# Linear attention with decay and a bilinear FFN on one core: the second pair's loads, scalings, transposes and order of products are changed

## The chip, the cores and the metric

The kernel runs on one core of a Trainium2 chip. The metric is the device time of one execution in microseconds (us). A core has five engines that run beside each other, each in the order of its own instructions: TensorE (PE in the profile; PEld is its loading of weights), VectorE (DVE), ScalarE (ACT), GpSimd (POOL) and SyncE (SP), which here issues nearly all transfers. An instruction waits on semaphores for what it needs, and everything behind it on its engine waits with it. SBUF is the memory that the engines work on; PSUM, eight banks of 2 KB a partition, takes TensorE's results.

## The reference

Two stages. The first is attention with a state that decays, for 4 batches, 8 heads, 768 tokens and 64 values a head; the second a bilinear FFN on all 3072 tokens.

```python
gamma = 1.0 - 2.0 ** (-5.0 - np.arange(H))
for t in range(S):
    state = gamma * state + einsum('bhd,bhe->bhde', k[:, :, t], v[:, :, t])
    y[:, :, t] = scale * einsum('bhd,bhde->bhe', q[:, :, t], state)
x = y.transpose(0, 2, 1, 3).reshape(B * S, H * D)      # 3072 x 512
out = ((x @ w_a) * (x @ w_b)) @ w_out                  # 512 -> 1536 -> 512
```

## The kernel before, in words

**The attention, by chunks.** Tokens are taken in slots of 128 (24 slots, six to a batch). The decay is put into k and q beforehand: `scaled` (L203) multiplies the raw tile by a table and writes bf16 into `kqb`. v is only cast to bf16 (`vb`). Then, for each slot: the scores, a product of k and q transposed (`at`); their masking on VectorE into `aT`; the state (`st` in PSUM), to which a product of k and v is added; a bf16 copy of the state; and `y`, the sum of an inter product (old state with q) and an intra product (masked scores with v). `y` is copied as bf16 into `xt`, the FFN's input, tokens along the free side.

**The first six slots go in pairs.** For batch 0, `load_pair` (L93) loads 256 tokens of k, q or v at once, 512 KB: partition p holds tokens 2p and 2p+1 ("par" 0 and 1). So a tile of parity par holds every second token. `casts2` (L331) does a pair's scalings and v's casts, with the engine named for k and q, and v's casts on GpSimd right behind. `flip2` (L339) transposes k and q on TensorE into PSUM and copies them to SBUF: `kT2` by parity, `qT2` with the two parities woven together, so that its tokens stand in order. `scores2` (L354) multiplies k of one parity with q of all 256 tokens in halves c of 128 tokens and masks the result with `masks[par]`. `update2(u, c)` (L373) adds half c of a pair to the state; `keep_state` (L390) copies the state to `gbd[1 - c]` with two ScalarE instructions. `inter2` (L394) multiplies `gbd[c]` with q, `intra2` (L405) v with the masked scores, and `leave2` (L417) casts `ys[u][c]` into `xt`. `warm` (L429) is a product of zeros that nothing reads; it keeps TensorE occupied. From slot 6 on the slots are handled one at a time, from slot 10 on with transposes made by transfers.

**PSUM.** The pool `psff` has three buffers, handed out in turn to transposes, scores of one parity, and all FFN products; `psat` and `psst` hold the other scores, `y` and the state.

**The order is written out by hand.** `seq` (L73) ties each instruction to the one before it on its engine, so lines 508 to 581 are the order on every engine for the three pairs and the FFN's first tile, in which `ffn_a` (a = x w_a, copied to `asb` by ScalarE) and `ffn_g` (g = x w_b, times `asb` on VectorE into `ht`) run over 12 blocks ft of 128. For ft 0 and 1 they run on half of the tile's columns at a time: the first 256 columns are pair 0's tokens, the others pair 1's. The weights are cast to bf16 on GpSimd (`cast_w`, `cast_o`) as they land. From L584 `run` follows for the other tiles, with `turn` for the attention of later slots in between and `ffn_out` (L472) for the outputs.

**The queue of transfers.** `LOADS` (L21) is the order of the first loads on SP's queue; `issue_loads(6)` issues the first entries at L123, the rest comes at L542. Later loads are issued by `casts` behind the transposes of a slot. A transfer waits for the one eight places before it in the program's order, as they share a semaphore in turn; that counts the stores too, of which the first six are issued by SP and the later ones by ScalarE, behind the copy of the output that they store.

## Time and profile before

| What | us |
|---|---|
| median of 3 timed executions | 233.76 (233.73 to 234.46) |
| the profiled execution, its own time | 235.14 |
| span of its instructions | 233.40 |
| TensorE busy in the span | 226.59 |
| VectorE, ScalarE, GpSimd busy | 95.65, 84.53, 77.43 |

The columns of the page are explained where they are used. In an order of time, a row has the start in us, the length in us, the engine, the line of the kernel, the operation, the tiles as output<-input, the shape, how many instructions are merged into the row, and in brackets how long the engine had been idle before and what released it. A table of stretches has, for each, its length, then the busy time of PE, PEld, DVE, ACT and POOL with the count of instructions, the clock granted to TensorE (1.00 is full), the share of the transfer engines and GB/s. A row of groups has the busy time and the mean of one in ns, then the idle time before them. Rows that begin with a start and a length and have no tile's shape are pieces of the chain of waits: the work that ended last, followed back.

### The profile page before, as it was taken

The numbers are of one execution on the slowest core, as the hardware profiler recorded it, in microseconds if no ns is written. First come the engines' busy times: TensorE is split into PE (matmuls) and PEld (weight loads), VectorE is DVE, ScalarE is ACT, GpSimd is POOL, SyncE is SP. The second block draws the span as 40 slices with busy tenths as digits, with TensorE's granted clock in tenths as the row PEclk, the third lists the DMA queues.
The fourth block names the chain that finished last, engine by engine and source line by source line (L and its number), as shares of the span: only waits on it lengthen the run. The fifth ranks groups of instructions, "written<-read, shape, count | busy, mean of one in ns | idle before, by whom it ended". The sixth has DMA issues, their size and how long they took to land.

```text
span 233.4 us, 5089 instructions
## 1 busy us (share of the span) xinstructions
PE 226.6 (97%) x2094; PEld 125.8 (54%) x2094; DVE 95.7 (41%) x170; ACT 84.5 (36%) x166; POOL 77.4 (33%) x100
## 2 busy tenths in 40 slices
PE   7999999999999999999799999999999999999995
PEld 6667445686554444545354544454544444445874
DVE  3785267543642274614164630164720233310530
ACT  3454436342134433414244523353422343322422
POOL 4347666788664336444454530000000000000000
PEclk9999999999999999999999999999999999999999
DMA  6999999999999999999999972200002200012102
GB/s 173 290 332 352 341 278 361 363 212 222 204 195 263 277 217 228 177 220 220 249 243 203 234 113 90 93 1 3 0 3 90 90 0 3 0 45 90 48 0 90
DMA packets 91894, 38.59 MB, mean 165 GB/s; under 512 B 71776, under 2 KB 87392, under 8 KB 91872
## 3 DMA queue, kind: packets, MB, share of 16 engines
q1 hardware_dynamic: 89280, 33.69, 64.8%
q10 hardware_dynamic: 2592, 4.59, 5.9%
q8 instruction: 16, 0.26, 0.5%
q14 instruction: 6, 0.05, 0.1%
HBM read 28.31 MB, written 6.29 MB: 148 GB/s over the span
## 4 chain that ended last, share of the span: by engine, by line
PE 74%; DMA 10%; SPq 7%; POOL 3%; ACT 1%; issue 1%; DVE 1%; ACTq 0%; POOLq 0%
PE g L456 22%; PE a L446 21%; PE o L481 19%; DMA kf<-in_k_dram 8%; SPq L223 4%; PE idle L432 4%; SPq L91 3%; POOL kqb L209 3%; DMA qf<-in_q_dram 2%; PE at L252 1%; PE y L297 1%; PE y L412 1%; PE tp L348 1%; PE st L268 1%; PE at L364 1%
## 5 line engine op out<-in xcount | busy, mean ns | idle before, releaser
L458 DVE TENSOR_TENSOR ht<-g,asb 128x512 bf16<-128x512 f32 (+1 forms) x86 | 52.0, 605 | 108.9 <-PE g L456 83.7
L456 PE MATMUL g<-xt,wb_bf 128*128 128x512 bf16 (+1 forms) x344 | 75.4, 344 | 1.6 <-ACT asb L449 1.4
L446 PE MATMUL a<-xt,wa_bf 128*128 128x512 bf16 (+1 forms) x344 | 75.9, 345 | 0.4 <-DVE xt L181 0.3
L449 ACT CAST asb<-a 128x512 bf16<-128x512 f32 (+1 forms) x86 | 44.2, 517 | 72.2 <-PE a L446 69.1
L481 PE MATMUL o<-wo_bf,ht 128*128 128x512 bf16 (+2 forms) x312 | 64.2, 363 | 0.0
L456 PEld LDWEIGHTS <-wb_bf 128*128 128x128 bf16 x344 | 33.6, 98 | 30.2 <-issue 2.1
L446 PEld LDWEIGHTS <-wa_bf 128*128 128x128 bf16 x344 | 32.7, 98 | 28.1 <-DVE xt L181 0.6
L481 PEld LDWEIGHTS <-ht 128*128 128x128 bf16 x312 | 29.2, 98 | 31.5
L209 POOL TENSOR_TENSOR kqb<-kf,ktab 128x512 bf16<-128x512 f32 x22 | 22.9, 1043 | 33.9 <-DMA kf<-in_k_dram 33.4
L179 ACT COPY osb<-o 128x512 f32<-128x512 f32 (+2 forms) x25 | 14.1, 565 | 53.5 <-PE o L481 41.5
L257 DVE TENSOR_TENSOR aT<-at,mask 128x512 bf16<-128x512 f32 x36 | 22.3, 682 | 0.0
L209 POOL TENSOR_TENSOR kqb<-qf,qtab 128x512 bf16<-128x512 f32 x18 | 18.8, 1043 | 3.9 <-DMA qf<-in_q_dram 3.1
L181 POOL CAST vb<-vf 128x512 bf16<-128x512 f32 x24 | 14.5, 612 | 11.6 <-DMA vf<-in_v_dram 9.8
L432 PE MATMUL idle<-zero 128*128 128x256 f32 x30 | 10.4, 487 | 1.6 <-DVE zero L125 1.3
L306 ACT CAST xt<-y 128x512 bf16<-128x512 f32 x18 | 9.7, 589 | 3.0 <-PE y L297 3.0
L432 PEld LDWEIGHTS idle<-zero 128*128 128x128 f32 x30 | 6.7, 243 | 2.9 <-DVE zero L125 1.2
L370 DVE TENSOR_TENSOR aT<-at,mask 128x512 bf16<-128x512 f32 x12 | 7.4, 683 | 1.2 <-PE at L364 1.2
L181 POOL CAST wa_bf<-wsta 128x1024 bf16<-128x1024 f32 (+1 forms) x7 | 6.4, 920 | 3.5 <-DMA wsta<-in_moe_w_a_dram 3.5
L181 POOL CAST wb_bf<-wstb 128x1024 bf16<-128x1024 f32 (+1 forms) x7 | 6.4, 920 | 3.4 <-DMA wstb<-in_moe_w_b_dram 3.4
L181 POOL CAST wo_bf<-wsto 128x1024 bf16<-128x1024 f32 x6 | 6.3, 1042 | 2.4 <-DMA wsto<-in_moe_w_out_dram 2.4
L179 ACT CAST gst<-st 128x256 bf16<-128x256 f32 x12 | 4.5, 372 | 6.7 <-PE st L268 6.7
L252 PE MATMUL at<-kqT 64*64 64x128 bf16 x288 | 5.8, 219 | 0.0
(51 smaller groups left out, 86.8 us busy)
## 6 DMA issues: line engine op xcount, KB each, us to landing
kf<-in_k_dram SPq DMA_DIRECT2D x18, 256.0 KB, 4.3
qf<-in_q_dram SPq DMA_DIRECT2D x18, 256.0 KB, 4.9
vf<-in_v_dram SPq DMA_DIRECT2D x18, 256.0 KB, 5.0
out_dram<-osb ACTq DMA_DIRECT2D x17, 256.0 KB, 2.0
wsta<-in_moe_w_a_dram SPq DMA_DIRECT2D x6, 512.0 KB, 8.7
wstb<-in_moe_w_b_dram SPq DMA_DIRECT2D x6, 512.0 KB, 8.7
wsto<-in_moe_w_out_dram SPq DMA_DIRECT2D x6, 512.0 KB, 9.4
kf<-in_k_dram SPq DMA_DIRECT2D x3, 512.0 KB, 7.1
```

The source lines that it names most:

```text
L179: seq(nc.scalar.copy(dst, src))
L181: seq(engine.tensor_copy(dst, src))
L209: seq(eng.tensor_tensor(dst, src, tab, op=ALU.mult))
L223: seq(nc.sync.dma_start_transpose(out=kqT[t].rearrange("p a b c -> p (a b) c"), in_=kqb[t].rearrange("p a hp r d -> p (a hp r d)")))
L257: seq(nc.vector.tensor_tensor(aT[t][:, r], at[r], mask.to_broadcast([P, HP, P]), op=ALU.mult))
L306: seq(nc.scalar.copy(xt[J][:, 2 * r : 2 * r + 2, i * P : (i + 2) * P].rearrange("p j (s n) -> p j s n", s=2), ys[t // 2][r].rearrange("p ( ...
L432: seq(nc.tensor.matmul(idle[:, : 2 * P], zero[:, :P], zero, start=True, stop=True, skip_group_check=True))
L446: seq(nc.tensor.matmul(a, wa_bf[:, kt, fs], xcols(J, kt, c0, c1), start=(kt == 0), stop=(kt == KT - 1)))
L449: seq(nc.scalar.copy(asb, a))
L456: seq(nc.tensor.matmul(g, wb_bf[:, kt, fs], xcols(J, kt, c0, c1), start=(kt == 0), stop=(kt == KT - 1)))
L458: seq(nc.vector.tensor_tensor(ht[J][:, ft, c0:c1], g, asbs.pop((J, ft, c0)), op=ALU.mult))
L481: seq(nc.tensor.matmul(o, ht[J][:, ft, i * P : (i + 1) * P], wo_bf[:, ft, c0:c1], start=(ft == 0), stop=(ft == NFT - 1)))
```

## The change

Names and lines here are those of the kernel before.

- The first loads are listed one by one, and k of pair 1 goes ahead of v of pair 0: k0, q0, k1, v0, q1, v1.
- GpSimd scales k of pair 1 first and casts v of pair 0 after that; q of pair 1 is scaled by VectorE (parity 0) and GpSimd (parity 1), where VectorE did both.
- `flip2` keeps q's transposes by parity, as k's, so that the copies write side by side; `scores2` and `inter2` read q with the two parities one after the other; the masks are built in that order; `leave2` weaves the parities together as it writes `xt`.
- The order by hand: after pair 0's scores come pair 1's k transposes, and pair 0's and pair 1's products are interleaved anew; the state copies for pair 0 come later; all products of pair 1 stand before the first `ffn_a`, and one warm-up product of a single call is left out. One copy of pair 0's `y` is on VectorE instead of ScalarE.

```diff
-LOADS = "p0 p1 w0 w1 w2 w3 w4 p2 w5 o0 ... s11".split()
+LOADS = "k0 q0 k1 v0 q1 v1 w0 w1 w2 w3 w4 k2 q2 v2 w5 o0 ... s11".split()
...
-    issue_loads(6)
+    issue_loads(10)
...
-                                        base=-par, pattern=[[0, 1], [1, P]],
+                                        base=-par, pattern=[[0, 1], [1, 2], [2, 64]],
...
     def casts2(u, on):
-        for t in (2 * u, 2 * u + 1):
-            new_nat(t)
+        if 2 * u not in kqb:
+            for t in (2 * u, 2 * u + 1):
+                new_nat(t)
         for (i, par), eng in on.items():
-            scaled(eng, 2 * u + par, i)
-        for t in (2 * u, 2 * u + 1):
-            cast(nc.gpsimd, vb[t], raws["v", t])
+            t = 2 * u + par
+            if i == V:
+                cast(eng, vb[t], raws["v", t])
+            else:
+                scaled(eng, t, i)
...
     def flip2(u, i, on):
-        if i == 1 and u not in qT2:
-            qT2[u] = tra.tile([P, HP, P, 2], BF16, tag="qT2", name="qT2", bufs=2)
+        into = (kT2, qT2)[i]
+        if u not in into:
+            into[u] = tra.tile([P, 2, HP, P], BF16, ...)
...
-                cast(eng, qT2[u][:, :, :, pars[0]], tp[:, 0])
+            cast(eng, into[u][:, pars[0] : pars[0] + len(pars)], tp)
...
-                                         qT2[u][half(r), hp, half(c), :],
+                                         qT2[u][half(r), :, hp, half(c)],
...
-                                         qT2[u][:, hp, half(c), :], start=False, stop=False,
+                                         qT2[u][:, :, hp, half(c)], start=False, stop=False,
...
-            cast(eng, xt[J][:, i + c], ys[u][c])
+            cast(eng, xt[J][:, i + c].rearrange("p k (m par) -> p k par m", par=2),
+                 ys[u][c].rearrange("p k (par m) -> p k par m", par=2))
...
     casts2(0, {(K, 1): D_, (K, 0): D_, (Q, 0): D_, (Q, 1): D_})
+    casts2(1, {(K, 0): G_, (K, 1): G_})
+    casts2(0, {(V, 1): G_, (V, 0): G_})
...
     scores2(0, 1)
     scores2(0, 0, True)
+    warm(2, psat, "y1")
+    flip2(1, K, [((0, 1), A_)])
+    intra2(0, 1, True)
     update2(0, 0)
-    warm(2, psat, "y1")
-    casts2(1, {(K, 0): G_, (K, 1): G_, (Q, 0): D_, (Q, 1): D_})
+    intra2(0, 0, False)
+    casts2(1, {(Q, 0): D_, (Q, 1): G_, (V, 0): G_, (V, 1): G_})
+    flip2(1, Q, [((0,), D_)])
+    inter2(0)
+    flip2(1, Q, [((1,), A_)])
+    leave2(0, (D_, A_))
     update2(0, 1)
-    intra2(0, 1, True)
-    inter2(0)
-    intra2(0, 0, False)
-    flip2(1, K, [((0, 1), A_)])
-    leave2(0, (A_, A_))
-    flip2(1, Q, [((0,), D_), ((1,), D_)])
-    warm(1, psff, "ff")
     scores2(1, 0, True)
     scores2(1, 1)
+    warm(2, psff, "ff")
     update2(1, 0)
+    intra2(1, 0, True)
+    inter2(1)
+    update2(1, 1, False)
+    intra2(1, 1, False)
+    leave2(1, (A_, D_))
     cast_w(0, 2)
     W2 = 2 * P
-    warm(2, psff, "ff")
-    update2(1, 1, False)
-    intra2(1, 0, True)
-    inter2(1)
     ffn_a(0, 0, 0, W2)
-    intra2(1, 1, False)
-    leave2(1, (A_, D_))
     ffn_a(0, 1, 0, W2)
...
+    ffn_a(0, 1, W2, 2 * W2)
     ffn_g(0, 1, 0, W2)
-    ffn_a(0, 1, W2, 2 * W2)
...
-            casts2(2, {(K, 0): G_, (K, 1): G_})
+            casts2(2, {(K, 0): G_, (K, 1): G_, (V, 0): G_, (V, 1): G_})
```

More of the change, by code (lines that the diff above doesn't have):

```diff
@@ L18 @@
 ON_PE = 10
-LOADS = "p0 p1 w0 w1 w2 w3 w4 p2 w5 o0 o1 o2 o3 o4 o5 s6 s7 s8 s9 s10 s11".split()
+LOADS = "k0 q0 k1 v0 q1 v1 w0 w1 w2 w3 w4 k2 q2 v2 w5 o0 o1 o2 o3 o4 o5 s6 s7 s8 s9 s10 s11".split()
 @with_exitstack
@@ L91, in load_slot, with load_pair @@
             seq(nc.sync.dma_start(out=raws[nm, t], in_=s))
-    def load_pair(u):
-        for nm, src in (("k", k), ("q", q), ("v", v)):
-            f = raw.tile([P, H, 2, D], F32, tag=nm + "f", name=nm + "f")
-            s = src[0, :, 2 * u * P : 2 * (u + 1) * P, :].rearrange("h (p two) d -> p h two d", two=2)
-            seq(nc.sync.dma_start(out=f, in_=s))
-            for par in range(2):
-                raws[nm, 2 * u + par] = f[:, :, par, :]
+    def load_pair(nm, u):
+        src = {"k": k, "q": q, "v": v}[nm]
+        f = raw.tile([P, H, 2, D], F32, tag=nm + "f", name=nm + "f")
+        s = src[0, :, 2 * u * P : 2 * (u + 1) * P, :].rearrange("h (p two) d -> p h two d", two=2)
+        seq(nc.sync.dma_start(out=f, in_=s))
+        for par in range(2):
+            raws[nm, 2 * u + par] = f[:, :, par, :]
     def load_w(j):
@@ L118, in issue_loads @@
             what = pending.pop(0)
-            {"p": load_pair, "s": load_slot, "w": load_w, "o": load_o}[what[0]](int(what[1:]))
+            if what[0] in "kqv":
+                load_pair(what[0], int(what[1:]))
+            else:
+                {"s": load_slot, "w": load_w, "o": load_o}[what[0]](int(what[1:]))
     kqb = {}
-    issue_loads(6)
+    issue_loads(10)
     zero = const.tile([P, 2 * P], F32, name="zero")
@@ L331, in casts2 @@
     def casts2(u, on):
-        for t in (2 * u, 2 * u + 1):
-            new_nat(t)
+        if 2 * u not in kqb:
+            for t in (2 * u, 2 * u + 1):
+                new_nat(t)
         for (i, par), eng in on.items():
-            scaled(eng, 2 * u + par, i)
-        for t in (2 * u, 2 * u + 1):
-            cast(nc.gpsimd, vb[t], raws["v", t])
+            t = 2 * u + par
+            if i == V:
+                cast(eng, vb[t], raws["v", t])
+            else:
+                scaled(eng, t, i)
     def flip2(u, i, on):
-        if i == 0 and u not in kT2:
-            kT2[u] = tra.tile([P, 2, HP, P], BF16, tag="kT2", name="kT2", bufs=2)
-        if i == 1 and u not in qT2:
-            qT2[u] = tra.tile([P, HP, P, 2], BF16, tag="qT2", name="qT2", bufs=2)
+        into = (kT2, qT2)[i]
+        if u not in into:
+            into[u] = tra.tile([P, 2, HP, P], BF16, tag="kq"[i] + "T2", name="kq"[i] + "T2", bufs=2)
         for pars, eng in on:
```

5 lines of the change are left out of this document (1 added, 4 removed).

## The prediction

> **What bounds the kernel now.** I read the page's busy times and its chain of waits first, then the stretches, then the order of time on each engine in the two places where TensorE is not full.
>
> ```profile
> span 233.4 us, 5089 instructions
> PE 226.6 (97%) x2094; PEld 125.8 (54%) x2094; DVE 95.7 (41%) x170; ACT 84.5 (36%) x166; POOL 77.4 (33%) x100
> PE 74%; DMA 10%; SPq 7%; POOL 3%; ACT 1%; issue 1%; DVE 1%; ACTq 0%; POOLq 0%
> ...
> 100.00:150.00 50.00, 48.76 (x426) 23.69 (x425) 16.76 (x27) 16.85 (x31) 18.70 (x21) 1.00 0.96 190
> 150.00:200.00 50.00, 50.00 (x388) 23.90 (x387) 18.98 (x29) 18.56 (x34) 0.00 (x0) 1.00 0.06 22
> ```
>
> TensorE is busy 97%, in the two stretches shown at full clock (the 1.00). But the chain is only 74% TensorE: 17% of it is transfers and SP's queue. From 150 us on TensorE is full; the one hole after 24 us lies between 100 and 150 (48.76 of 50). The change works on the first 23 us, where warm-up matmuls hide the waits. So there are two questions: what the front gains, and whether the hole swallows it. The chain at the hole, then PE and ACT there:
>
> ```profile
> 109.18 5.36 DMA qf<-in_q_dram
> 114.61 0.34 ACTq L491
> 114.99 0.59 ACT asb L449
> ...
> 115.63 1.02 PE L456 MATMUL g<-xt,wb_bf 128*128 128x512 bf16 x4 [1.24 <-ACT asb L449]
> ...
> 111.83 0.59 ACT L179 COPY osb<-o 128x512 f32<-128x512 f32 x1 [2.00 <-PE o L481]
> 114.99 0.59 ACT L449 CAST asb<-a 128x512 bf16<-128x512 f32 x1 [2.57 <-DMA qf<-in_q_dram]
> ```
>
> The output copy ends at 112.42, its store stands behind it on ScalarE's queue, and the store is issued only when a load of q, issued at 109.18, has landed (114.54). The asb copy queued behind the store holds g: TensorE loses 1.24 us. Nothing later on TensorE waits, so the end is 114.54 plus fixed work, whenever TensorE comes there earlier, and also when it comes up to 1.24 us later. What sets 114.54 is the train of loads, transposes and stores on SP's queue. The change swaps two entries of that queue (k of pair 1 and v of pair 0, equal sizes) and leaves its other entries and their order alone.
>
> **The front, part by part.** Times are those of the trace.
>
> ```profile
> 8.64 0.70 PE L432 MATMUL idle<-zero 128*128 128x256 f32 x2
> 9.63 0.64 PE L364 MATMUL at<-qT,kT 64*64 64x128 bf16 x32 [0.29 <-DVE qT L181]
> 15.22 0.76 PE L364 MATMUL at<-qT,kT 64*64 64x128 bf16 x32
> 19.28 0.61 PE L446 MATMUL a<-xt,wa_bf 128*128 128x256 bf16 x4
> 20.18 0.61 PE L446 MATMUL a<-xt,wa_bf 128*128 128x256 bf16 x4 [0.29 <-DVE xt L181]
> ...
> 8.84 0.73 DVE L181 COPY qT<-tp 128x512 bf16<-128x512 bf16 x1 [0.60 <-PE tp L348]
> 10.10 2.48 DVE L370 TENSOR_TENSOR aT<-at,mask 128x512 bf16<-128x512 f32 x4 [0.53 <-PE at L364]
> ...
> 10.55 0.76 ACT L392 CAST gbd<-st 64x256 bf16<-64x256 f32 x2 [1.69 <-PE st L383]
> 13.53 1.01 ACT L179 COPY kT<-tp 128x1024 bf16<-128x1024 bf16 x1 [0.80 <-PE tp L348]
> ...
> 8.72 1.17 POOL L181 CAST vb<-vf 128x512 bf16<-128x512 f32 x2 [4.77 <-DMA vf<-in_v_dram]
> 10.62 2.04 POOL L209 TENSOR_TENSOR kqb<-kf,ktab 128x512 bf16<-128x512 f32 x2 [0.73 <-DMA kf<-in_k_dram]
> ...
> 4.95 1.74 SPq L97 DMA_DIRECT2D qf<-in_q_dram  x1
> qf<-in_q_dram SPq DMA_DIRECT2D x1, 512.0 KB, 7.3
> ...
> 16.23 1.06 PE idle L432 x4
> 17.89 0.57 PE y L400 x16
> 19.00 0.40 PE y L412 x16
> 21.66 0.44 PE a L446 x4
> ```
>
> These are, in this order, TensorE, VectorE, ScalarE, GpSimd, the issue of pair 1's q with its time to landing, and four pieces of the chain.
>
> *Transposes by parity.* The copy out of PSUM now writes side by side instead of every second element.
>
> ```profile
> L458 DVE TENSOR_TENSOR ht<-g,asb 128x512 bf16<-128x512 f32 x58 | 40.1, 691 | 86.4 <-PE g L456 72.2 <-ACT asb L449 14.2
> L458 DVE TENSOR_TENSOR ht<-g,asb 128x256 bf16<-128x256 f32 x28 | 11.9, 425 | 22.6 <-PE g L456 11.5 <-ACT asb L449 11.1
> L238 DVE COPY kqT<-tp 128x1024 bf16<-128x1024 bf16 x4 | 2.8, 689 | 3.6 <-PE tp L236 3.6
> L179 ACT COPY qT<-tp 128x512 bf16<-128x512 bf16 x2 | 1.5, 738 | 0.5 <-PE tp L348 0.5
> L179 ACT COPY kT<-tp 128x512 bf16<-128x512 bf16 x2 | 1.1, 588 | 1.9 <-PE tp L348 1.9
> ```
>
> On ScalarE that is 738 to 588 ns. On VectorE the two ht rows give (691 - 425)/256 = 1.04 ns an element and 159 ns fixed; kqT, 1024 elements side by side, has (689 - 159)/1024 = 0.52 ns. So qT with 512 takes about 159 + 265 = 424 ns instead of 730 (bounds: 345, half of kqT's row, and no gain). The scores of pair 0 then start at 9.34, when the warm-up matmuls end, not at 9.63: -0.29, and aT ends at 12.30 instead of 12.58. The strided write moves to xt, 588 to 738 ns at worst; the a products of the first half cover it (0.88 us on TensorE), or it costs 0.15.
>
> *k ahead of v.* GpSimd gets k when it got v, 8.72, and is done at 10.76; v follows to 11.93, two microseconds later than now. Its readers are queued later as well: the scores (0.64) end at 9.98, the warm-ups (1.06) at 11.0, k's transposes at about 11.6, ScalarE's kT copy (1.01) at 12.6, and the state copies of keep_state (0.76) stand behind it, to 13.4, where now they end at 11.31. inter2(0) waits for those; behind it on TensorE stands the second half of q's transposes.
>
> *q on two engines.* q lands at 4.95 + 7.3 = 12.25, unmoved. The likely price comes from these rows (DVE, then POOL):
>
> ```profile
> 34.05 0.82 DVE L209 TENSOR_TENSOR kqb<-qf,qtab 128x512 bf16<-128x512 f32 x1
> 12.50 1.32 DVE L209 TENSOR_TENSOR kqb<-qf,qtab 128x512 bf16<-128x512 f32 x2
> 35.39 0.68 DVE L458 TENSOR_TENSOR ht<-g,asb 128x512 bf16<-128x512 f32 x1
> ...
> 32.27 2.04 POOL L209 TENSOR_TENSOR kqb<-kf,ktab 128x512 bf16<-128x512 f32 x2 [0.69 <-DMA kf<-in_k_dram]
> ```
>
> VectorE's scaling began at 34.05 while GpSimd's ran to 34.31, and took 0.82, where the pair at 12.50 took 0.66 each: it ended 0.55 after GpSimd did, as if it had stood still until then. Side by side the two halves may thus come one after the other.
> (a) GpSimd first, 12.35 to 13.39; VectorE ends at 13.94; transposes 14.35, inter2 14.6, second half 14.9, ScalarE's copy 0.59, scores of pair 1 at 15.55: +0.33 on 15.22.
> (b) VectorE first, 13.03, GpSimd (1.04) 14.07, transposes 14.45, copy 15.05, scores 15.1: -0.1.
> (c) No exclusion: GpSimd 13.39, inter2 done 13.85, transposes 14.1, copy 14.7, scores 14.77: -0.45.
> I take (a), since both times that the trace shows the pair it is VectorE that stands.
>
> [...]
>
> *All products first.* From the scores of pair 1 to the first a of the second half (15.22 to 20.18) TensorE has the same work, in another order. Now the last a before it starts at 19.28 and needs 0.44, so 0.46 is waiting for xt, which goes, since two a (0.88) stand behind the last intra while xt is copied (0.69 to 0.74). New is a wait inside inter2(1): its state update now follows the warm-up, and its copies (0.76 and about 0.1 of hand-over) have only intra (0.40) and the first half of inter (0.29) as cover: 0.17. Uncovered whole it would be 0.86. Net -0.3. The masking of aT, 2.48 long, ends before its last reader as now.
>
> Front in all: (a) 0.0, (b) -0.4, (c) -0.75. A further limit stands at pair 2:
>
> ```profile
> 36.20 0.78 PE L348 MATMUL tp<-ident,kqb 128*128 128x128 bf16 x8
> 37.09 1.02 PE L456 MATMUL g<-xt,wb_bf 128*128 128x512 bf16 x4
> ```
>
> The transposes at 36.20 need the PSUM buffer that ht frees at 35.39 + 0.68 = 36.07, and that ht follows the scaling tied to k's landing at 32.2, which doesn't move. After 36.07 only ScalarE's chain shortens, so g at 37.09 can come to about 36.6: at most -0.5 goes on. At 115 the 0.0 to 0.5 meets the unmoved 114.54: the 1.24 us wait becomes up to 1.74.
>
> Sum: 233.4 span + 0.0 = 233.4. The profiled execution took 235.14 (1.74 around its span), the median without a profile is 233.76; no change there too, rounded **233.7**.
>
> **Rivals.** *R1, the hole is not there without a profile.* The profiled execution is 1.38 longer than the median, nearly the hole's 1.24; against it, the instants of the loads come from kernel queues that are the same in both. Then the front goes through: 233.76 - 0.0 to 0.5, 233.3 to 233.7.
> *R2, faster.* (c) holds, the hole is absent, and pair 2 gives way as well (its scaling is no longer beside GpSimd's k if the transfers run quicker): 233.76 - 0.75 = 233.0. Its case is weakened by the 0.82 row.
> *R3, slower: a store overtakes the load.* ScalarE issues the third store of this block at 109.86, 0.68 after the q load at 109.18. If TensorE arrives over 0.68 earlier, 256 KB stand ahead of that load:
>
> ```profile
> 108.00:114.50 6.50, 6.39 (x30) 2.81 (x29) 0.01 (x1) 1.17 (x2) 2.05 (x3) 1.00 1.03 185
> ```
>
> at 185 GB/s that is 1.4 us, and 114.54 becomes 115.9: 235.1. The limit of 0.5 at pair 2 speaks against it.
> *R4, the split does not do what it says.* By (a) q takes 1.04 + 0.55 = 1.59 instead of 1.32; the gain of the other parts is spent on it. It ends at 233.7 with or without the hole, so it is inside the forecast.
>
> **How the numbers follow.** What a measurement of this kernel can tell from no change is about 0.3%, 0.70 us: same is 233.06 to 234.46. The hole absorbs (with R4): 0.47. R1: 0.14. R2 and larger gains: 0.22. R3, or a train of transfers that is later for another reason: 0.17. From the first two nearly all is same, 0.59; faster 0.23, slower 0.18. The likeliest case alone has 233.3 to 234.1; with the top of R2 and about half of R3's price, 232.9 to 234.5.
>
> **What would show it.** Right: the wait before g near 115 grows by what the front gains, the q load still lands near 114.5, and the end stands. For the front: VectorE's qT copy near 0.42; GpSimd's and VectorE's q scalings, one of them longer than its 1.04 or 0.66; the scores of pair 1 at 15.1 to 15.6; the first a of the second half at 19.8 to 20.2. Wrong: no wait near 115 and an end shorter by the front's gain, or a load of q that lands elsewhere than at 114.5 by more than 0.5.

## The result, and the profile after

| | before | after |
|---|---|---|
| median of 20 timed executions, us | 234.08 | 234.70 |
| shortest | 233.58 | 234.59 |
| profiled execution, its own time (span) | 235.14 (233.4) | 234.88 (233.2) |

The ratio is 1.0028, with a 95% interval of 1.0015 to 1.0041: the change made the kernel 0.6 us slower, where 233.7 and no change had been forecast. Single executions lie up to 1.9 us apart for before and 0.9 for after, and one of each, some 4 us longer, is left out of the ratio, so the shortest of each, 1.01 us apart, is shown beside the median.

The page of after: span, busy times, the engines' shares of the chain of waits, and two groups (busy us, mean ns, idle time ahead and what ended it).

```profile
span 233.2 us, 5085 instructions
PE 226.5 (97%) x2092; PEld 126.3 (54%) x2092; DVE 94.4 (41%) x169; ACT 84.5 (36%) x166; POOL 78.8 (34%) x101
PE 94%; DVE 2%; ACT 1%; issue 1%; ACTq 0%
L449 PE MATMUL a<-xt,wa_bf 128*128 128x512 bf16 (+1 forms) x344 | 75.7, 345 | 0.5 <-DVE ht L461 0.4
```

The chain is TensorE for 94%, where 17% had been transfers and SP's queue: the wait of 1.24 us near 115 is gone. TensorE's busy time is the same, and yet the span is only 0.2 less. The stretches of after say where TensorE stood instead (length, then busy PE, PEld, DVE, ACT, POOL, clock, DMA share, GB/s):

```profile
16.00:24.00 8.00, 7.38 (x146) 5.72 (x135) 4.70 (x9) 4.35 (x12) 5.01 (x7) 1.00 1.10 349
24.00:50.00 26.00, 25.45 (x235) 14.40 (x234) 13.57 (x24) 10.57 (x20) 18.11 (x19) 1.00 1.04 314
100.00:150.00 50.00, 50.00 (x433) 24.34 (x432) 17.21 (x27) 17.54 (x32) 18.73 (x21) 1.00 0.96 189
```

0.62 us is idle between 16 and 24, another 0.55 between 24 and 50, none between 100 and 150. Both places in order of time, with the front's rows that answer to the prediction's (VectorE and GpSimd first, then TensorE, then the second place):

```profile
9.54 0.42 DVE L184 COPY qT<-tp 128x512 bf16<-128x512 bf16 x1 [1.37 <-PE tp L353]
12.34 1.04 POOL L212 TENSOR_TENSOR kqb<-qf,qtab 128x512 bf16<-128x512 f32 x1 [0.45 <-DMA qf<-in_q_dram]
12.89 1.04 DVE L212 TENSOR_TENSOR kqb<-qf,qtab 128x512 bf16<-128x512 f32 x1
15.73 0.47 PE L366 MATMUL at<-qT,kT 64*64 64x128 bf16 x20 [0.31 <-ACT qT L182]
...
17.62 0.34 PE L414 MATMUL y<-aT,vb 64*64 64x128 bf16 x9
18.59 0.27 PE L414 MATMUL y<-aT,vb 64*64 64x128 bf16 x5 [0.62 <-issue]
18.79 0.64 PE L402 MATMUL y<-qT,gbd 128*64 128x128 bf16 x16
19.95 1.56 PE L449 MATMUL a<-xt,wa_bf 128*128 128x256 bf16 x12
21.35 0.60 PE L459 MATMUL g<-xt,wb_bf 128*128 128x256 bf16 x4
...
37.81 1.02 PE L459 MATMUL g<-xt,wb_bf 128*128 128x512 bf16 x4
39.35 0.69 DVE L461 TENSOR_TENSOR ht<-g,asb 128x512 bf16<-128x512 f32 x1 [1.57 <-PE at L366]
40.09 1.02 PE L449 MATMUL a<-xt,wa_bf 128*128 128x512 bf16 x4 [0.44 <-DVE ht L461]
```

The row of before that answers to after's `g` at 21.35:

```profile
20.62 1.04 PE L456 MATMUL g<-xt,wb_bf 128*128 128x256 bf16 x8
```

At 17.97, in the middle of `intra2(1, 0, True)`, TensorE stops for 0.62 us between two products that have the same inputs as their neighbours, and the row gives "issue": nothing that the profile shows held it. The first `a` of the second half starts 0.44 ahead of the `g` at 21.35, so at about 20.9; before had 20.18. The `a` at 40.09 has waited 0.44 for an `ht` that starts at 39.35, although both of its inputs, `asb` and `g` (which ends at 38.83), were there 0.5 earlier.

Near 115 the load that held before's store came at another time. ScalarE and SP's queue there in after:

```profile
112.96 0.59 ACT L182 COPY osb<-o 128x512 f32<-128x512 f32 x1 [2.00 <-PE o L484]
113.57 0.35 ACTq L494 DMA_DIRECT2D out_dram<-osb  x1
...
107.28 0.73 SPq L91 DMA_DIRECT2D qf<-in_q_dram  x1
```

The q load was issued at 107.28 and landed at 112.82, where before had 109.18 and 114.54. So it was there before the output copy ended (113.55), and the store followed its copy at once.

The trace has one more kind of event, which the views only count (queue q8, "instruction", 16 transfers of 16 KB in the span): at the start of the last three of them in before, TensorE had begun 3,483, 3,757 and 4,027 records, 274 and 270 apart; over all sixteen it is 247 in the mean, but unevenly (110 to 387). The first of the sixteen ran from 16.14 to 17.26 in after, and from 14.06 to 15.23 in before. The product that starts at 18.59 is TensorE's record number 449 (weight loads, products and semaphore events, counted from 0). From this came theory F: record 449 is the first whose code has to be fetched during the span, and TensorE stood waiting for code. (That queue q8 carries TensorE's code is part of the theory: the trace gives a transfer's queue, kind, size and times, not what it holds.)

### The profile page after: what moved, and what is told of

Its sections match the earlier page's. It is cut to its first block, busy times and chain, and to the rows that moved or that the text cites. A ratio compares the mean times of both kernels' runs of the same rounds, so it can differ in the third digit from the quotient of the medians.

```text
span 233.2 us, 5085 instructions
## 1 busy us (share of the span) xinstructions
PE 226.5 (97%) x2092; PEld 126.3 (54%) x2092; DVE 94.4 (41%) x169; ACT 84.5 (36%) x166; POOL 78.8 (34%) x101
## 4 chain that ended last, share of the span: by engine, by line
PE 94%; DVE 2%; ACT 1%; issue 1%; ACTq 0%
PE o L484 27%; PE g L459 27%; PE a L449 27%; PE idle L435 4%; PE at L255 2%; PE y L300 2%; PE st L271 2%; PE tp L353 1%; DVE aT L372 1%; PE y L291 1%; PE y L414 1%; PE y L402 1%; PE at L366 1%; PE tp L237 0%; ACT asb L452 0%
## 5 line engine op out<-in xcount | busy, mean ns | idle before, releaser
L182 ACT COPY osb<-o 128x512 f32<-128x512 f32 (+2 forms) x25 | 14.1, 565 | 53.5 <-PE o L484 39.7
L212 POOL TENSOR_TENSOR kqb<-qf,qtab 128x512 bf16<-128x512 f32 x19 | 19.8, 1044 | 4.3 <-DMA qf<-in_q_dram 3.9
```

Source lines behind the costliest of these rows:

```text
L182: seq(nc.scalar.copy(dst, src))
L212: seq(eng.tensor_tensor(dst, src, tab, op=ALU.mult))
```

## The experiments

All 18 kernels were run beside before on the same chip, each group on another one; before's shortest run was 233.63 to 233.69 on all of them. "Pause" is the time that TensorE stood right ahead of record 449, "code" the start of the first 16 KB transfer; both are from the trace of the profiled execution, us. "last" is the end of the last product.

| run | code | record 449 at | pause | idle at 39 to 42 | idle at 114 to 116 | last | shortest | median | ratio to before |
|---|---|---|---|---|---|---|---|---|---|
| before | 14.06 | 17.38 | none | none | 1.24 | 230.54 | 233.58 | 234.08 | |
| after | 16.14 | 18.59 | 0.62 | 0.44 | none | 230.25 | 234.59 | 234.70 | 1.0028 [1.0015, 1.0041] |
| x1 | 14.17 | 17.39 | none | none | 0.67 | 229.99 | 233.65 | 234.48 | 0.9979 [0.9946, 1.0012] |
| x2 | 15.99 | 18.61 | 1.52 | none | none | 229.92 | 234.23 | 235.07 | 0.9995 [0.9966, 1.0025] |
| x3 | 13.87 | 17.46 | none | 0.43 | none | 229.62 | 234.15 | 234.87 | 0.9980 [0.9955, 1.0005] |
| x4 | 13.26 | 16.94 | none | none | 2.36 | 232.95 | 233.35 | 235.48 | 1.0003 [0.9970, 1.0037] |
| y2 | 16.18 | 19.17 | none | none | none | 231.06 | 233.55 | 235.64 | 1.0014 [0.9975, 1.0052] |
| y3 | 16.39 | 18.85 | 1.08 | 0.43 | 0.84 | 231.10 | 234.46 | 234.71 | 1.0013 [0.9979, 1.0046] |
| y4 | 15.93 | 18.61 | 0.96 | 0.46, 0.44 | none | 232.55 | one run | 237.16 | |
| z1 | 13.29 | 15.90 | none | none | 1.59 | 230.47 | 234.27 | 235.14 | 1.0016 [0.9991, 1.0041] |
| z2 | 13.12 | 15.85 | none | none | 1.64 | 230.46 | 234.59 | 235.08 | 1.0026 [1.0001, 1.0052] |
| z3 | 17.73 | 20.38 | 1.35 | 0.44 | none | 232.04 | 236.66 | 236.93 | 1.0115 [1.0062, 1.0167] |
| w1 | 13.53 | 17.41 | none | none | none | 229.17 | 233.70 | 233.98 | 0.9967 [0.9941, 0.9993] |
| w2 | 15.93 | 18.61 | 0.59 | 0.44 | none | 230.28 | 234.35 | 234.61 | 0.9997 [0.9976, 1.0017] |
| w3 | 14.62 | 17.05 | 0.17 | none | none | 229.86 | 233.21 | 233.70 | 0.9960 [0.9936, 0.9984] |
| w4 | 13.13 | 15.87 | none | none | none | 230.44 | 233.21 | 233.55 | 0.9967 [0.9942, 0.9992] |
| v1 | 15.76 | 18.36 | 0.34 | none | 0.21 | 229.99 | 234.22 | 235.29 | 1.0017 [0.9987, 1.0047] |
| v2 | 14.87 | 18.09 | none | none | none | 229.85 | 233.67 | 235.04 | 1.0009 [0.9978, 1.0039] |

w3's pause is read from the distance of two warm-ups, 0.39 where z1, z2 and w4 have 0.21, since the earlier one still counts as busy. The clock granted to TensorE was 0.97 in the mean from 100 to 150 in x4's profile (half of it for 3.41 us from 117.22) and 0.58 from 20 to 24 in y4's (half from 19.93), so the ends of these two are not compared with the others'. y1 and z4, whose profiled executions were 2 and 3.5 times as long, are told of below.

### First four: parts alone

x1 is the kernel before, once more.

> The kernel before, unchanged. Theory HOLE (the prediction's): the wait of about 1.2 us before a g near 115 us belongs to the kernel and is there again, span about 233.4. Theory CHANCE (rival R1): the wait belongs to that one execution; here g near 115 waits under 0.3 us and the span is 231.9 to 232.4. Ratio 1.000 either way.

x2 takes the split of q out of after:

```diff
-    casts2(1, {(Q, 0): D_, (Q, 1): G_, (V, 0): G_, (V, 1): G_})
+    casts2(1, {(Q, 0): D_, (Q, 1): D_, (V, 0): G_, (V, 1): G_})
```

> The changed kernel with both of pair 1's q scalings on VectorE again, nothing else. Theory LOCK (the two scalings exclude each other, GpSimd first): they take 1.32 together instead of 1.59 and VectorE's starts at once, so the scores of pair 1 start 0.4 to 0.7 earlier than the 15.73 of the changed kernel and the time is 0.3 to 0.7 below it, ratio to before about 1.000 to 1.002. Theory ORDER (the loss lies behind the scores, in the new order of products and state copies): the time stays within 0.2 of the changed kernel, ratio about 1.003.

x3 puts the split alone into before:

```diff
-    casts2(1, {(K, 0): G_, (K, 1): G_, (Q, 0): D_, (Q, 1): D_})
+    casts2(1, {(K, 0): G_, (K, 1): G_, (Q, 0): D_, (Q, 1): G_})
```

> The kernel before with only the second q scaling of pair 1 moved to GpSimd, behind its k. LOCK: GpSimd's q runs 12.7 to 13.7 or waits for VectorE's, to 14.3, v's casts slip by up to 0.3, the scores of pair 1 start 0.1 to 0.4 later than 15.22: ratio 1.0005 to 1.002, and one of the two scalings is longer than its 1.04 or 0.68. No exclusion: both keep their lengths, ratio 0.999 to 1.000. ORDER says nothing here but that it is no more than 1.001.

x4 puts the layout by parity alone into before, with the masks, `inter2` and `leave2` that go with it:

```diff
-            qT2[u] = tra.tile([P, HP, P, 2], BF16, tag="qT2", name="qT2", bufs=2)
+            qT2[u] = tra.tile([P, 2, HP, P], BF16, tag="qT2", name="qT2", bufs=2)
...
-                                         qT2[u][half(r), hp, half(c), :],
+                                         qT2[u][half(r), :, hp, half(c)],
```

> The kernel before with only the layout by parity (q's transposes kept by parity, masks in that order, order restored in xt). The prediction's term: VectorE's qT copy 0.42 instead of 0.73, the scores of pair 0 start 0.29 earlier (9.34 for 9.63) where the warm-ups allow it; at the end of the front 0 to 0.4 less: ratio 0.998 to 1.000. If the strided write of xt (0.74 for 0.59) costs more than the copies give: 1.000 to 1.001.

x2 was the telling one. TensorE in its order of time:

```profile
14.85 0.64 PE L366 MATMUL at<-qT,kT 64*64 64x128 bf16 x32 [0.30 <-ACT qT L182]
16.74 0.34 PE L414 MATMUL y<-aT,vb 64*64 64x128 bf16 x9
18.61 0.27 PE L414 MATMUL y<-aT,vb 64*64 64x128 bf16 x5 [1.52 <-issue]
```

The scores of pair 1 came at 14.85, 0.88 earlier than in after, and the pause at the very same product grew by 0.90 and ended at the same instant (18.61, in after 18.59). Nothing of the data came later; something with a time of its own held the product. x1's hole was 0.67, between the two values expected, where before's had been 1.24: the q load behind it landed at 113.99 in place of 114.54. So that wait varies from one execution of a kernel to the next. x3's shortest run lay 0.5 over x1's, which nothing explained yet. x4's shortest was 233.35, 0.3 under x1's, as the 0.29 of the earlier scores would have it, but its interval covers 1. In its profile the scores of pair 1 came at 14.91, 0.31 ahead of before's, and `g` of the first half at 20.22, 0.40 ahead; all of it and more was lost at 115, where the q load landed at 115.26 and TensorE stood 2.36.

### Second four: is it a place in the code or a product?

y1 and y2 add records ahead of the place, in after and in x2's kernel:

```diff
+    def tiny(n, pool, tag):
+        idle = pool.tile([P, 4 * P], F32, tag=tag, name="idle")
+        for _ in range(n):
+            seq(nc.tensor.matmul(idle[:32, :1], zero[:, :32], zero[:, :1], start=True, stop=True, ...))
...
-    warm(6, psat, "y1")
+    warm(5, psat, "y1")
+    tiny(9, psat, "y1")
```

> The changed kernel with 32 more TensorE records ahead of the first k transposes: the last of the six warm-ups (4 records) is replaced by nine products of one column (36 records) that nothing reads. Theory F, code fetch: TensorE's 449th record in the span is the first whose code has to be fetched during the span (one 16 KB transfer on the instruction queue, 16.14 to 17.26 us, then 18.59 before it runs); the 0.62 us idle in intra of pair 1 is that wait. The wait then stands at record 449 again, which is 32 records earlier in the program (in the state product of pair 1 rather than in intra). Where the transfer is asked for at a record behind the q transposes' wait (258), it is now asked for ahead of that wait: transfer from about 14.5, no wait left, first a of the second half at 20.2, 0.5 to 0.7 us less than after (about 234.0). Where it is asked for at record 193 (256 less), it comes only about 0.2 earlier while TensorE reaches record 449 about 0.3 earlier: the wait stays, 0.6 to 0.9 us long, time within 0.3 of after (234.7). Rival S, data: the product at 18.59 waits for scores or state copies: the idle time stays at the same product of intra, 0.6 us, time that of after.

> As y1, with both q scalings of pair 1 on VectorE, so that scores of pair 1 start at 14.85 in place of 15.73. Theory F with the request behind record 258: transfer from about 14, done by 15.2, no wait; first a of the second half at about 19.4, time about 233.3, less than both. Theory F with the request at record 193: wait at record 449 (in the program 32 records earlier) of about 1.7 us, its end at about 18.4, time that of after (234.7). Rival S: as x2, idle of 1.5 us at the same product of intra, 234.7.

y3 joins warm-ups of 256 columns in pairs to products of 512 columns (`warm` with `cols=4 * P`, `zero` twice as wide); y4 adds `tiny` behind the scores of pair 1:

```diff
-    warm(6, psat, "y1")
+    warm(3, psat, "y1")
...
-    warm(2, psff, "ff")
+    warm(1, psff, "ff")
```

```diff
     warm(2, psff, "ff")
+    tiny(8, psff, "ff")
```

> The changed kernel with 24 fewer TensorE records ahead of intra of pair 1: the warm-ups in pairs are joined to products of 512 columns (4 records where two of 256 columns had 8; same TensorE time). Theory F: the wait is at record 449 again, 24 records later in the program (in inter of pair 1), and about 0.3 us of work is done ahead of it: 0.3 us of idle time is left if the transfer comes when it did, time 0.2 to 0.4 below after (about 234.4). Rival S: idle of 0.6 us at the same product of intra, time that of after.

> The changed kernel with 32 more TensorE records behind the scores of pair 1 (eight products of one column after the last two warm-ups), so behind any record that could ask for the code. Theory F: the transfer on the instruction queue starts when it did (about 16.1); idle time again at record 449, now 32 records earlier in the program (the end of the state product of pair 1), its end at about 18.6; the work behind it is 32 records longer, first a of the second half about 0.2 to 0.4 later than after's 20.8. Rival S: idle of 0.5 us at the same product of intra as in after, end at 18.6, first a at 20.8.

The pause, in y3 and then in y4:

```profile
17.36 0.41 PE L402 MATMUL y<-qT,gbd 128*64 128x128 bf16 x7
18.85 0.44 PE L402 MATMUL y<-qT,gbd 128*64 128x128 bf16 x9 [1.07 <-issue]
...
17.27 0.37 PE L385 MATMUL st<-vb,kqb 64*64 64x64 bf16 x11
18.61 0.22 PE L385 MATMUL st<-vb,kqb 64*64 64x64 bf16 x2 [0.96 <-issue]
```

With 24 records fewer it moved on into `inter2(1)`, with 32 more it moved back into `update2(1, 0)`: in the trace it stands at record 449 both times. That settles it against a wait for data, which would have stayed with its product. (y4's pause lies ahead of its stretch of lower clock.) The end followed the transfer: in the eight kernels with a pause (after, x2, y3, y4, z3, w2, v1 and, shortest, w3) record 449 runs 2.43 to 2.68 us after the transfer's start, in the others 2.61 or more. Fewer records did not help, since in y3's execution the transfer itself came at 16.39.

y1's and y2's filler did more than was meant. In y2's profile the whole front was late (pair 0's scores at 11.59, in after 10.01); TensorE came to record 449 only at 19.17, 2.99 us after the transfer's start, and had no pause; its shortest run, 233.55, is 1.0 under after's. y1's shortest was 233.75, but two of its 12 runs took 468 us, the profiled one among them.

### Third four: the same records at no cost

z1 and z2 (x2's kernel) give the warm-ups another form:

```diff
+    zb = const.tile([P, P], BF16, name="zb")
+    seq(nc.vector.memset(zb, 0.0))
...
+    def small(n, pool, tag):
+        idle = pool.tile([P, 4 * P], F32, tag=tag, name="idle")
+        for _ in range(n):
+            seq(nc.tensor.matmul(idle[:, :P], zb, zb, start=True, stop=True, ...))
...
-    warm(6, psat, "y1")
+    warm(1, psat, "y1")
+    small(40, psat, "y1")
```

z3 has k of pair 1 loaded behind v of pair 0 in after; z4 has z1's warm-ups in before.

```diff
-LOADS = "k0 q0 k1 v0 q1 v1 ...
+LOADS = "k0 q0 v0 k1 q1 v1 ...
```

> The changed kernel with the first six warm-ups (24 records, 5.1 us) made into one of them and 40 products of 128 x 128 in bfloat16 (84 records, the same 5.1 us of full use), so 60 more records early at no TensorE time. Theory F, code fetch: record 449, the first whose code comes during the span, is now 60 records earlier in the program (at the end of the scores of pair 1, which after's profile reached at 16.2), and record 193, whose passing asks for the code, is passed at about 10.2 in place of 12.3. With a delay of 1.8 to 4.2 us from asking to transfer, as in the runs so far, the transfer starts at 12 to 14.4 and its code runs 2.5 us later, at 14.5 to 16.9: between no idle time and 0.7 us of it, and none left at 17.97. First a of the second half at 20.2 (0.65 less than after), time about 234.0. Rival S, data: idle 0.6 us at the same product of intra of pair 1, time that of after (234.6). Rival T: the wait is moved only, 0.6 us or more elsewhere, time that of after.

> As z1, with both q scalings of pair 1 on VectorE (as in x2, where scores of pair 1 came 0.9 us earlier and the whole 0.9 us was idled away at record 449). Theory F: record 449 is reached at about 15.3; code there at 14.5 to 16.9: 0 to 1.6 us of idle time. Without idle time first a of the second half at about 19.4 and 0.7 to 0.8 us less than before (233.0); with all of it as after (234.6). Rival S: as x2, 1.5 us idle at the same product of intra, 234.6.

> The changed kernel with k of pair 1 loaded behind v of pair 0 again. GpSimd's order stays (k of pair 1, then v of pair 0), so GpSimd waits about 1.5 us more for k, and v of pair 0 comes that much later than in after: intra of pair 0 and all behind it 1 to 1.5 us later, scores of pair 1 at about 16.7 to 17.2. If the load order is what puts the code transfer at 16 in place of 14, the transfer is back at about 14, TensorE has no idle time at record 449, and the first a of the second half is at 21 to 21.5; if the load order has no part in it, the transfer stays at 16 to 16.4 and the code is there at 18.6, ahead of TensorE or 0.2 behind it. Time 0 to 0.7 above after (234.6 to 235.3).

> The kernel before with the same 60 more records early. Theory F: no idle time was there to be won, since TensorE reached record 449 at 17.4 with its code there from about 16.6; now it reaches it in the program 60 records earlier, at about 15.7 to 16.5, with the code there at 14.5 to 16.9: time that of before (233.7 to 234.0), 0.3 more at most. A rival that the filler changes something else (the clock, the first transposes) would show here as a change of the same size as in z1.

z1 in its order of time, TensorE and then ScalarE's queue:

```profile
15.01 0.64 PE L368 MATMUL at<-qT,kT 64*64 64x128 bf16 x32 [0.30 <-ACT qT L184]
16.91 0.40 PE L416 MATMUL y<-aT,vb 64*64 64x128 bf16 x14
17.24 1.06 PE L404 MATMUL y<-qT,gbd 128*64 128x128 bf16 x16
18.82 1.54 PE L457 MATMUL a<-xt,wa_bf 128*128 128x256 bf16 x12
20.21 0.60 PE L467 MATMUL g<-xt,wb_bf 128*128 128x256 bf16 x4
...
111.22 1.03 PE L457 MATMUL a<-xt,wa_bf 128*128 128x512 bf16 x4
115.57 1.02 PE L467 MATMUL g<-xt,wb_bf 128*128 128x512 bf16 x4 [1.59 <-ACT asb L460]
...
114.55 0.34 ACTq L502 DMA_DIRECT2D out_dram<-osb  x1
114.93 1.07 ACT L460 CAST asb<-a 128x512 bf16<-128x512 f32 x2 [2.92 <-DMA qf<-in_q_dram]
```

The pause is gone and `intra2(1, 0, True)` runs through (14 products without a gap). `g` at 20.21 is 0.41 ahead of before's 20.62 and 1.14 ahead of after's 21.35. All of the lead is then lost at 115, where the store behind the q load is issued at 114.55, as in before (114.61): the hole grew to 1.59. z2 did the same. So taking the pause away did not yet make the kernel faster.

z3 missed its expectation: 1.15% slower. With the order of GpSimd's work as it is, k behind v puts the scores of pair 1 at 16.79, and the first 16 KB transfer came later too, at 17.73, 3.9 us after TensorE had passed record 193 (256 less than 449); in after it was 3.85. (That record 193 asks for the transfer is an assumption that no run shows; the 256 is an estimate, beside the mean of 247 records between transfers in before.) So the transfer came later as TensorE did, and the old order of the loads did not bring it back to 14. Its delay after record 193 was 1.8 to 2.5 us in before, x1, x3, x4 and w1, 2.7 in y2, and 3.1 to 4.3 in after, x2, y3, y4, z1 to z3, w2 to w4, v1 and v2. What makes that difference was not found.

z4's shortest run was 233.93 and its ratio 1.0004 (0.9973 to 1.0034): before gains nothing from the earlier records, as expected. One of its 12 runs, the profiled one, took 816.8 us.

### Fourth four: the store out of the way

In w1 (before), w2 (after), w3 (z1) and w4 (z2) the last output store of the third block is issued two `asb` copies later on ScalarE's queue:

```diff
             if J < 2:
                 held.append((dst, src))
+            elif (J, i) == (2, 3):
+                late.append((dst, src))
...
     def ffn_ab(J, ft):
         store()
         ffn_a(J, ft)
         ffn_g(J, ft)
+        if ft == 1 and late:
+            dst, src = late.pop()
+            seq(nc.scalar.dma_start(out=dst, in_=src))
```

> The kernel before with one output store moved: the fourth of the third block, which stands on ScalarE's queue ahead of two asb copies and waits for the landing of a q load near 114.5, is issued two asb copies later. Theory H, hole: in before's profiled executions that wait cost TensorE 1.24 and 0.67 us, so this kernel has no idle time of TensorE at 114 to 116, and its time is that of the shortest runs of before in nearly all its runs: median 233.5 to 233.9 against 234.1 to 234.7 for before beside it. Rival: the wait only passes on to another copy or load, time unchanged.

> The changed kernel with the same store moved. Theory F and H together: after had the idle time at record 449 (0.62 us) and none at 115, because TensorE comes there 0.65 later; moving the store changes nothing it waits for: 234.5 to 234.7, idle time at record 449 as in after, ending at 18.6. Rival: after loses its time at the store in the runs that are not profiled: then 233.7 to 234.0.

> z1 (the changed kernel, 60 more records early, no idle time at record 449) with the same store moved. z1 reached the first a of the second half 0.42 earlier than before's profile and gave all of it back in 1.59 us of idle time at 114 to 115.6. Theory F and H: no idle time at either place, TensorE at 112 us 0.4 ahead of before and 1.1 ahead of after: 233.1 to 233.5, less than both. Rival: the idle time goes to the next wait for a load (kqT of the next slots), time 233.9 or more.

> z2 (as z1, q of pair 1 on VectorE alone) with the same store moved. z2's scores of pair 1 came at 14.96 and z1's at 15.01, so it is expected to end with w3: 233.1 to 233.5; idle time nowhere over 0.4 us between 16 and 215. Rival: as w3's.

w1's stretches and two of its rows, then two rows of w3 at 115:

```profile
24.00:50.00 26.00, 25.86 (x242) 15.08 (x241) 14.55 (x24) 10.85 (x21) 18.08 (x20) 1.00 1.06 316
100.00:150.00 50.00, 50.00 (x433) 24.34 (x432) 17.15 (x27) 17.51 (x32) 18.57 (x21) 1.00 0.90 188
...
20.21 0.61 PE L446 MATMUL a<-xt,wa_bf 128*128 128x256 bf16 x4 [0.28 <-DVE xt L181]
111.67 1.03 PE L446 MATMUL a<-xt,wa_bf 128*128 128x512 bf16 x4
...
115.15 0.59 ACT L460 CAST asb<-a 128x512 bf16<-128x512 f32 x1 [1.14 <-PE a L457]
115.21 0.34 ACTq L477 DMA_DIRECT2D out_dram<-osb  x1
```

The hole is gone in all four, and the times move as theories F and H (the hole belongs to that store) had them. before gains (ratio 0.9967, median 233.98 against 234.44 for before beside it), after does not (0.9997), and after without the pause gains (0.9960 and 0.9967). w3 and w4 are the shortest kernels of the study: 233.21 in their shortest runs, 0.49 under w1's 233.70 and 1.14 under w2's 234.35. Their medians, 233.70 and 233.55, lie 0.3 to 0.4 under w1's, less than the intervals can tell apart, and above the 233.1 to 233.5 that was expected. w3's profile missed its expectation too: GpSimd scaled first there, the scores of pair 1 came at 15.99, `g` of the first half at 21.35 as in after, and its last product ended 0.69 behind w1's. In w4's profiled execution, the longest of its 12 runs, TensorE stood 1.44 us at 78.9 behind an output copy that waited for an earlier store to land.

Against w1, the profile of before without the hole, after can be added up. `g` of the first half is at 21.35 against 20.66 in w1: 0.69 later. The second idle time adds 0.41 (25.45 us busy between 24 and 50, in w1 25.86). That is 1.10, and the last product ends 1.08 later (230.25 against 229.17).

### Last two: the second idle time

The idle time of `a` at 39 to 42 stood in after, x3, y3, y4, z3 and w2, with a late `ht` ahead of it each time, and in none of the others. (y4's other one, 0.46 at 39.65, is of a transpose that waits for another `ht`.) Those six have 281 VectorE records in the trace, as one scaling of q is on GpSimd; the others have 282 or 283 (the split with one memset more, or no split). In all six it is record 63 that starts 0.46 or 0.47 us after record 62, a semaphore event that had already passed. v1 (after) and v2 (x3) add nothing but `zb` and its memset, one VectorE instruction:

> The changed kernel with one more VectorE instruction early (a memset of a tile that nothing reads, about 0.1 us). Theory V, VectorE's code: in every kernel with one q scaling of pair 1 on GpSimd (281 VectorE records in the profile) VectorE's 64th record, the first ht of pair 2's stretch, starts 0.41 to 0.47 us after its inputs, and the next a of TensorE 0.41 later; in every kernel with 282 or 283 that place stands one record earlier or more and falls into a wait. With the memset: no idle time of TensorE at 39.7, the idle time at record 449 unchanged (end at 18.6), last product 0.4 earlier (about 229.9), shortest runs about 234.2 in place of 234.6. [...]

> x3 (the kernel before with one q scaling of pair 1 on GpSimd) with the same memset. Theory V: x3's shortest runs lay 0.5 us over before's (234.15 against 233.65) because its 64th VectorE record met the same pause (38.24 to 38.70); with the memset the pause at ht is gone, the last product is 0.4 earlier than x3's 229.62, and the shortest runs are back at 233.7. [...]

VectorE and TensorE in x3, then in v1:

```profile
38.70 0.69 DVE L458 TENSOR_TENSOR ht<-g,asb 128x512 bf16<-128x512 f32 x1 [1.26 <-PE at L364]
39.45 1.02 PE L446 MATMUL a<-xt,wa_bf 128*128 128x512 bf16 x4 [0.43 <-POOL wb_bf L181]
...
37.58 1.02 PE L461 MATMUL g<-xt,wb_bf 128*128 128x512 bf16 x4
38.71 0.69 DVE L463 TENSOR_TENSOR ht<-g,asb 128x512 bf16<-128x512 f32 x1 [1.17 <-PE g L461]
39.45 1.02 PE L451 MATMUL a<-xt,wa_bf 128*128 128x512 bf16 x4
```

In v1 `ht` follows `g` at once and `a` has no idle time; the shortest run is 234.22, as expected (234.2), against 234.59. v2's shortest is back at 233.67, before's own (233.69 beside it). The medians of that chip were too scattered to show 0.4 us, and neither interval leaves 1 out, so it is the profiles and the shortest runs that carry this. The pause went with the count of VectorE's records (63 in all six), and one unread memset ahead of it took the idle time of `a` away. That it is a fetch of code, as theory F has it for TensorE, is argued from the likeness alone; no transfer was tied to it. (In the row of x3 the releaser is given as GpSimd's cast; that had nothing to do with it, since the idle time went with the memset.)

## Why the prediction was wrong

The forecast was a front of 0.0 and a hole that takes up whatever is left. Against w1, the front cost 0.69 and the place behind it 0.41, and in after's profile there was no hole. The parts, in the prediction's order:

**Transposes by parity: the prices right.** VectorE's copy of q's transposes took 0.42 (424 ns worked out), ScalarE's 0.59, the strided write of `xt` 0.72 to 0.75 (0.738). The scores of pair 0, forecast at 9.34 for 9.63, came at 9.36 in x2 and 9.42 in x4, but at 10.01 in after: the forecast took the end of the warm-ups as given, and it moves. The passes of the first warm-ups start 0.43 us apart and later 0.21. The step came at 4.3 in x2 and at 5.9 in before; in after the last of the first six still ran at 0.43. The clock records of these three traces, which the views only average, begin at 4.24, 5.72 and 7.48.

**q on two engines: the prices right, the choice partly luck.** (a) was taken, GpSimd first and VectorE done 0.55 after it: after shows GpSimd from 12.34 to 13.38 and VectorE done at 13.93. The lengthening goes both ways: VectorE's scaling took 1.04 there, where one of the same shape took 0.68 in after at 34.77, with no scaling on GpSimd beside it, and in z1, which shows (b), VectorE was first and GpSimd's took 1.48, where before's 18 of q took 1.04 in the mean:

```profile
12.29 0.69 DVE L214 TENSOR_TENSOR kqb<-qf,qtab 128x512 bf16<-128x512 f32 x1
12.41 1.48 POOL L214 TENSOR_TENSOR kqb<-qf,qtab 128x512 bf16<-128x512 f32 x1 [0.46 <-DMA qf<-in_q_dram]
```

The order differs between executions: (a) in after, w2, w3, v1 and v2, (b) in x3, y3, y4 and z1, (c) in none. In the kernels built on after it goes with the warm-ups: GpSimd's scaling starts 0.1 us behind q's landing, at 12.34 to 12.60, and VectorE comes from its masks of pair 0 at 12.67 to 13.13 in the four with (a) and at 12.36 to 12.39 in the three with (b). So choosing (a) was right for after's profile, and the reason given, that VectorE always stands, was not the one. The scores of pair 1 were predicted at 15.55 for (a) and 15.1 for (b); measured 15.73 in after and 15.01 in z1. R4's price of 1.59 for the two scalings was measured so in after (12.34 to 13.93); x2, without the split, had 1.29. What makes one scaling lengthen the other no run shows.

**All products first: the step that failed.** It said that from the scores of pair 1 to the first `a` of the second half "TensorE has the same work, in another order", net -0.3. Counted to the `g` behind that `a`, before took 5.40 us (15.22 to 20.62), after 5.62 (15.73 to 21.35), z1 5.20 (15.01 to 20.21). So in place of -0.3 the step cost +0.22. Without the pause the order is worth -0.20 (z2 took 5.19, w4 5.20): the mechanism holds, with the new wait in `inter2(1)` larger than the 0.17 that was reckoned, since its 16 products spread over 1.06 us in z1 and 0.64 in after. What the step left out is the pause. TensorE's small products, 9 in 0.34 us, brought it to record 449 at 17.97, 1.83 us after the first 16 KB transfer's start, and in the kernels with a pause that record ran 2.43 to 2.68 us after it. Before came to it at 17.38, 3.32 us after its transfer's start, and did not stand. By theory F the pause is a wait for code. No row of before shows that as a wait, and none gives its price; the instruction queue's line on the page (16 transfers, 0.5%) was the one sign.

**The second missed term** is the 0.41 us at 39.7, which moving one instruction off VectorE brought with it.

**The limit at pair 2** did not bind: z1's lead over w1 was 0.45 at `g` of the first half (20.21 against 20.66) and 0.45 at 111 (111.22 against 111.67).

**The hole at 115: its mechanism right, its fixed instant and its weight wrong.** Where the load lands at the same time, the hole grows as TensorE comes earlier: z1 waited 1.59 where before waited 1.24, the q load landing at 114.47 and 114.54. But the step "the end is 114.54 plus fixed work" failed. That load landed at 113.99 in x1, which is before once more, at 112.82 in after, at 112.32 in w3 and 115.26 in x4. In after it held nothing. So the prediction's own sign of being wrong was there: a landing more than 0.5 away from 114.5. What moves the train of transfers between executions was not found. The forecast gave 0.47 to the hole absorbing everything, because it took the profiled execution as typical. Before's shortest run is 1.56 less than it (233.58 against 235.14); x1's hole was 0.67; w1, without it, has a shortest run of 233.70, no shorter than before's own. So before's shorter runs most likely have no hole, and the front's difference goes through, as rival R1 had it. R1 was given 0.14 and only gains; what went through was a loss of 1.1 between the profiles. That the medians differ by 0.62 and the shortest runs by 1.01 fits with a hole in some runs of before and none in after's, but only profiled executions can show it.

**R3**, a store that overtakes the load, was not put to the test by after or z1, whose store was issued behind the load (109.44 and 108.98 in z1). In x4's profile it did go ahead: the third store at 109.46, the q load at 110.08, its landing at 115.26 (0.72 behind before's) and the longest hole of all. That the store was the reason is not shown, since the k load ahead of it on the queue was late by itself (109.45, in before 107.72).

## What to carry to other kernels

Here short products in a row (9 in 0.34 us) brought TensorE to record 449 up to 1.52 us before it ran (x2). So when idle time says "issue" and ends at the same instant whatever the data do, count the engine's records up to it, and move it by adding or leaving out records elsewhere. If it stays with the count, put records where the engine waits anyway; here 60 of them made of existing warm-ups, with one store moved, turned 0.3% slower into 0.4% faster. (Moving the store alone made before 0.3% faster; that the changed front adds to this is not shown.) And a wait of 1 us in one profiled execution of a kernel whose timed runs are spread by as much is not a wait that every run has (1.24 us in before, 0.67 in x1, the same kernel), and the instant at which a transfer lands in it is not fixed (112.32 to 115.26 here): profile it again before letting it absorb anything.

## What the runs showed of the hardware

- The queue that the page calls "instruction" (q8) moved 16 KB at a time, 16 times in the span, each in 0.88 to 1.74 us in before and after. In the eight kernels with a pause on TensorE, record 449 ran 2.43 to 2.68 us after the first transfer's start, and the pause was 0.17 (w3) to 1.52 us (x2); before, which came to that record 3.32 us after the start, had none. That the transfers hold TensorE's code is theory F, which the runs agree with and do not show directly.
- VectorE's record 63 started 0.46 or 0.47 us after its record 62 in each of the six kernels in which that place fell on an instruction with its inputs ready.
- Where a trace holds clock records, the first, of a granted clock of 1.00, begins between 4.24 us (x2) and 7.57 (w3), and at 10.33 in y2. In the kernels built on after that load k of pair 1 early, the scores of pair 0 came at 9.36 to 9.46 where that record begins by 6.28, and at 9.60 to 10.17 where it begins at 6.38 to 7.57.
- In a few runs TensorE stayed slow to the end: 2 of 12 runs of y1 took 468 us and 1 of 12 of z4 took 817. The views give a granted clock of 1.00 for them, but their traces hold no record of the clock, so that is no measurement. y1's `g` products took 604 ns in the mean and z4's 958, against 344 in after. y1 and z4 share only new forms of the first warm-ups, but z1, z2, w3 and w4 had z4's form in 48 runs without one such run, so the cause stays open.
